# One more chunk by seven products, with operand sums made by transfers, and new due dates, in the last batch of an attention and feed-forward kernel

## The chip, the cores and the metric

The kernel runs on one core of a Trainium2 chip. Its matrix engine (TensorE, PE in the profile) multiplies a loaded 128 x 128 weight by a stream of columns and adds into banks of PSUM; each bank holds 128 rows of 512 numbers in 32 bits. VectorE (DVE) and ScalarE (ACT) read those banks; GpSimd (POOL) works within SBUF here and issues the loads from DRAM; SyncE (SP) issues the stores and the transposes. The metric is the device time of one execution in microseconds; the time before is the median of three executions.

## What the kernel computes

There are two stages. The first is cross-covariance attention over the channels, for B = 4 batches with N = 5824 tokens and C = 256 channels. The second is a feed-forward of d_ff = 1024 without any nonlinearity but a product of two linear maps.

```python
qn = q / (norm(q, axis=1) + 1e-06)          # along the 5824 tokens
kn = k / (norm(k, axis=1) + 1e-06)
s = kn.transpose(0, 2, 1) @ qn / tau        # 256 x 256 per batch
a = softmax(s, -1)
x = (v @ a).reshape(23296, 256)

h = (x @ w1) * (x @ w2)                     # 23296 x 1024
out = (h @ w3) @ w_out                      # w3: 1024 x 1024, w_out: 1024 x 256
```

The inputs and the output are float32; the kernel's matmuls take bf16 operands and add in 32 bits.

## The kernel before, in words

**The algebra.** Two products are folded ahead. w3 @ w_out becomes W_sb, 1024 x 256, once. For every batch a @ w1 and a @ w2 become Wf[b] (256 x 1024 each, index w = 0 and 1), once the batch's scores G = q^T k, the norms and the softmax are known. So what is left for a token is a = v Wf[b] w=0, b = v Wf[b] w=1, abh = a * b, and o = abh W_sb. While batch b is at this, the loads and scores of the next batch run between; the last batch, b = 3, has none beside it.

**Tiling.** A batch is cut into 12 chunks (c = 0 to 11) of 512 tokens, the last of 192 columns; d_ff is cut into 8 blocks (j = 0 to 7) of 128. v is turned by transposing transfers that SP issues, two chunks together (`turned_v`).

**The first product, block by block.** `normal` (L986 to L1022) takes one block of one chunk: 2 matmuls 128 x 512 for a and 2 for b (L993), a cast of a by ACT (`as`, L983) and a multiplication by DVE into the tile abh (L1015). In batch 3 the chunks go in pairs (0,1), (2,3), (4,5), (6,7), (8,9), and some blocks of a pair are made by `by_seven` (L1026 to L1075) instead: a product of 2 x 2 blocks with 7 multiplications in place of 8, so 7 matmuls 128 x 512 (L978; into banks named X, Y, T and Z) for two chunks' a and b. It takes sums of the weights (`wsum`, made once) and sums of tokens (`tsum`, four POOL operations per pair, `token_sum`, L680 to L686), and DVE does four operations for it, two of them additions out of the banks. `BY_SEVEN` (L552) says how many of the eight blocks of a pair go that way.

**The second product, chunk by chunk.** When all eight blocks of a chunk are done, `queue_out` queues its product with W_sb, in one of two forms. `plain_products` has 8 steps, each of 4 matmuls 128 x 256 (`emit_half`, L1087), copied out by two ACT operations in batch 3 and stored by one transfer on SP. `seven_products` (L756 to L884) uses the same trick of 7 for 8: 7 steps, each of 8 matmuls 128 x 128 (L828; banks prodA, prodB, prodC), sums of W_sb's quarters (`comb_T`), and four sums S of the chunk's own abh. POOL makes these four sums, 128 x 1024 each (L788 for the first, L790 for the others, in two tiles S0 and S1). ACT copies the products out (`keep`, L841; the copy that seeds prodB, L858), DVE adds to them (`join`, L848), and SP stores the chunk (L882). A list `PLAIN` (L554) says which chunks take the plain form; in batch 3 these are 0, 2, 6, 9 and 10. The last chunk, 11, is emitted block by block, and so is 10.

**A third form that is in the code but not in use.** For a chunk in `BY_DMA` (L555, empty) the four sums are made by transfers within SBUF: SP issues two plain copies (L806, L807) and POOL issues four transfers that add what they read to what they write (`by_transfer`, L798). The second and third wait for the first to land, the fourth waits for the third. Two of the additions write over parts of the chunk's own abh. Since a transfer can add but not subtract, this form works with other signs: three of the four sums of W_sb are taken negated (`comb_N`, three POOL operations of 128 x 512, `negate_weights`, L741), and for half of the chunk's rows ACT multiplies by -1 on the way out of the bank (L839) and DVE subtracts (L846).

**What sets the order.** The program of every engine is fixed when the kernel is built. `step` (L1406) plays the engines forward with estimated costs (`now`, `work_on`) and at each turn chooses among a `normal` block (its start plus `N_BIAS`), up to two `by_seven` blocks, and the next step of the second product (plus `O_BIAS`, when there is no hurry). POOL's work lies in a list; `pool_due` (L621) issues, of what may go, the item with the least due time. The due time of a chunk's sum is the number of steps of second products ahead of it times `STEP`; that of a token sum is `SLOT` times `TOKENS_AHEAD` blocks less `T_EARLY`. `plan` (L1376) lays out the blocks of a batch, and among them the places of the `by_seven` blocks and, `TOKENS_AHEAD` blocks before a pair, the place at which its token sums are queued. `LANDING` (2.8) is what the planner takes for a transfer within SBUF. POOL also issues the loads of v, each behind a small copy that waits for a block of the product (the gate).

Of the kernel before, what the change touches and what calls it, by code (L numbers as in the profile page):

```python
# [11 lines left out]
F32 = DT.float32  # L12
BF16 = DT.bfloat16

P = 128
# [2 lines left out]
BIG_BUFS = 31  # L18
HALF_BACK = 12
LANDING = 2.8  # L20
STEP = 1.55
SLOT = 1.45
T_EARLY = 1.0
N_BIAS = 0.04
O_BIAS = 0.15
MM_COL = 1.0 / 2400.0
MM_FIX = 0.0025

# [2 lines left out]
def kernel(  # L31
# [12 lines left out]
    nc = tc.nc  # L44
# [28 lines left out]
    work = ctx.enter_context(tc.tile_pool(name="work", bufs=2))  # L73
# [475 lines left out]
        )  # L549


    BY_SEVEN = {(3, 0): 3, (3, 2): 4, (3, 4): 4, (3, 6): 4, (3, 8): 4}  # L552
    PAIRED = {b: tuple(c for b2, c in sorted(BY_SEVEN) if b2 == b) for b in range(B)}
    PLAIN = {0: (0, 1, ), 1: (), 2: (), 3: (0, 2, 6, 9, 10, )}  # L554
    BY_DMA = {3: ()}  # L555
    TSUM, WSUM0, TSUM0 = 100, 12.0, 26.0
    wsums = {}
    tsums = {}
# [2 lines left out]
    now = {"PE": 0.0, "ACT": 0.0, "DVE": 0.0, "POOL": 0.0}  # L561
# [6 lines left out]
    def work_on(engine, cost, *after):  # L568

        now[engine] = max(now[engine], *after, 0.0) + cost  # L570
        return now[engine] + LATE[engine]
# [36 lines left out]
    def pool_add(due, item):  # L608

        pool_line.append((*item, due))  # L610

    def steps_until(key, step):

        n = step
        for line in outs:
            if line.key >= key:
                return n
            n += line.left
        return n
# [34 lines left out]
    def queue_token_sums(b, c):  # L654

        until = now["PE"] + TOKENS_AHEAD * SLOT

        def step(i):
            def fn(at_):
                token_sum(b, c, i)  # L660
                if i == 3:
                    tready[b, c] = at_
            return fn

        for i in range(4):
            pool_add(
                lambda i=i: until - now["PE"] + 1.1 * (i - 3) - T_EARLY,
                (0.0, lambda: turned_at.get((b, c // 2), FAR) <= now["PE"], 1.06, step(i)),
# [87 lines left out]
    def seven_products(b, c, k1, k2, whole):  # L756
# [8 lines left out]
        my_key = out_key(b, c)  # L765
        if c not in BY_DMA.get(b, ()):
            summed.append(line_key)
# [3 lines left out]
        def first_line():  # L771
            return min(summed) if (b, c ^ 1) in summed or c % 2 == 0 or (b, c - 1) in was or c - 1 in PLAIN.get(b, ()) else None

# [20 lines left out]
        def by_transfer(i):  # L794
            def fn(at_):
                s3, s2 = sums["t"][:, 0], sums["t"][:, 1]
                dst, src = {3: (s3, a21), 1: (a21, a22), 2: (s2, s3), 4: (a12, s2)}[i]
                nc.gpsimd.dma_start(out=dst, in_=src, accum_op=ALU.add)  # L798
                sums[i] = dst
                made[i] = at_ + LANDING  # L800
            return fn

        by_dma = c in BY_DMA.get(b, ())
        if by_dma:
# [5 lines left out]
            for i, allowed in (  # L810
# [5 lines left out]
                pool_add(  # L816
                    lambda i=i: steps_until(my_key, {3: 2, 1: 3, 2: 2, 4: 6}[i]) * STEP - {3: 7.5}.get(i, 4.0),
                    (whole, allowed, 0.55, by_transfer(i)),
                )
        for i in range(1, 1 if by_dma else 5):  # L820
            pool_add(lambda i=i: steps_until(my_key, {1: 2, 2: 2, 3: 4, 4: 6}[i]) * STEP - 2.1, (whole, (lambda i=i: (i == 1 and sums_live[0] < 2 and first_line() == line_key) or (i > 1 and i - 1 in made)), 2.1, sum_step(i)))

# [65 lines left out]
    def plain_products(b, c, ab2, whole):  # L888

        for i in range(FT):  # L890
            yield lambda i=i: max(out_bank(f"out{i // 4}", whole), w_made[0])
            emit_half(b, c, i, ab2)
# [22 lines left out]
    def out_key(b, c):  # L915
        return b, c + 1.5 * (c in BY_DMA.get(b, ()) and c in PAIRED[b])

    def put_out(b, c, gen, steps):
        line = Line(gen)
        line.key = out_key(b, c)  # L920
        line.left = steps
        k = len(outs)
        while k > 1 and outs[k - 1].key > line.key:
            k -= 1
        if k == 1 and outs[0].key > line.key and not outs[0].begun:
            k = 0
        outs.insert(k, line)
        steps_left[0] += steps

    def queue_out(b, c, whole):  # L930

        ab2 = tuple(halves[c])
        queued[b] = queued.get(b, 0) + 1
        if c in PLAIN.get(b, ()):
            put_out(b, c, plain_products(b, c, ab2, whole), FT)
# [90 lines left out]
    def by_seven(b, c, j):  # L1026

        W = Wf[b]
        js = slice(j * P, (j + 1) * P)
        yield lambda: max(  # L1030
            bank_at(4), wready.get(b, FAR), tready.get((b, c), FAR), whole_at(2)
        )
        T = tsums[b, c]
        S = [wsums[b][h][:, x, :] for h in range(2) for x in range(2)]
        xt, X = take(f"X_{b}_{c}_{j}", True)
        r = mm512(X, W[:, 0, 0, js], rhs_of(b, c, 0), True)
        yt, Y = take(f"Y_{b}_{c}_{j}", True, True)
        nc.scalar.copy(Y, X)
        copied = work_on("ACT", 0.475, r, free.get(yt, 0.0))
        yield lambda: bank_at()  # L1040
        tt, t = take(f"T_{b}_{c}_{j}")
        r = mm512(t, S[0][:, js], T[:, 0], True)
        t5 = work.tile([P, 512], F32, tag="t5", name=f"t5_{b}_{c}_{j}", bufs=2)
        nc.scalar.copy(t5, t)
        t5_at = free[tt] = work_on("ACT", 0.475, r)
        yield lambda: max(copied, whole_at(1))
        r = mm512(X, S[1][:, js], T[:, 1], False)
        zt, Z = take(f"Z_{b}_{c}_{j}", True, True)
        nc.vector.tensor_add(Z, X, t5)
        z_at = work_on("DVE", 0.607, r, t5_at, free.get(zt, 0.0))  # L1050
        yield lambda: copied
        r = mm512(Y, W[:, 1, 0, js], rhs_of(b, c, 1), False)
        a0 = cast(Y, f"as_{b}_{c}_{j}")
        a0_at = free[yt] = work_on("ACT", 0.475, r)
        held.discard(yt)
        yield lambda: z_at
        r = mm512(X, S[2][:, js], T[:, 2], False)
        b1 = work.tile([P, 512], BF16, tag="b_sb", name=f"bs_{b}_{c + 1}_{j}", bufs=2)
        nc.vector.tensor_add(b1, X, t5)
        b1_at = work_on("DVE", 0.61, r)  # L1060
        yield lambda: z_at
        r = mm512(Z, S[3][:, js], rhs_of(b, c + 1, 1), False)
        h1 = place(b, c + 1, j)
        nc.vector.tensor_mul(h1, two_halves(b1), two_halves(Z))
        free[zt] = work_on("DVE", 0.6, r, b1_at)
        held.discard(zt)
        finish(b, c + 1, j, free[zt])
        yield lambda: b1_at
        r = mm512(X, W[:, 1, 1, js], T[:, 3], False)
        h0 = place(b, c, j)  # L1070
        nc.vector.tensor_mul(h0, two_halves(a0), two_halves(X))
        free[xt] = work_on("DVE", 0.6, r, a0_at)
        held.discard(xt)
        last_ab[:] = [h0, free[xt]]
        finish(b, c, j, free[xt])  # L1075
# [95 lines left out]
    for nm in "kq":  # L1171
        new_piece(nm, 0, 0)
        raw[nm] = work.tile([P, half, C], F32, tag="o_sb", name=f"raw_{nm}", bufs=3)
        first = nc.sync if nm == "k" else nc.scalar
# [131 lines left out]
    def make_agenda(b):  # L1306
# [42 lines left out]
        if b == 0:  # L1349
            for i in range(4):  # L1350
                at(COMB + COMB_STEP * i, 0.0, lambda i=i: combine_weights(i))
        if b == min((m for m in BY_DMA if BY_DMA[m]), default=-1) - 1:
            at(90, 0.0, negate_weights)
# [22 lines left out]
    def plan(b):  # L1376

        todo, sevens = [], []
        c = 0
        if b == 0:  # L1380
            todo += [(c, h * 4 + j) for h in range(2) for c in range(2) for j in range(4)]
            c = 2
        while c < NCH:
            if c in PAIRED.get(b, ()):
                k = BY_SEVEN[b, c]
                mine = [(2 * i + 1) * FT // (2 * k) for i in range(k)]
                rest = [j for j in range(FT) if j not in mine]
                first = len(todo)
                todo += [(c + d, j) for j in rest for d in range(2)]
                n = len(todo) - first  # L1390
                sevens += [(first + max(0, i * n // k), c, j) for i, j in enumerate(mine)]
                if c > 0:
                    token_at[b, max(0, first - TOKENS_AHEAD)] = c
                c += 2
            else:
                todo += [(c, j) for j in range(FT)]
                c += 1
        return todo, sevens

    TOKENS_AHEAD = 5  # L1400
    token_at = {}
    stuck = [0]
    credit = [0.0]
# [2 lines left out]
    def step(b, todo, sevens, at_n):  # L1406
# [14 lines left out]
        if lines["N"] is not None:  # L1421
            choices.append((max(now["PE"], lines["N"].est()) + N_BIAS, 3, lines["N"]))
        if outs:
            hurry = credit[0] > 0.0 or steps_left[0] > 2 * HALF_BACK or not todo
            choices.append((max(now["PE"], outs[0].est()) + (-0.02 if hurry else O_BIAS), 4, outs[0]))
        if not choices:
# [25 lines left out]
    for b in range(B):  # L1452
# [3 lines left out]
        todo, sevens = plan(b)  # L1456
# [10 lines left out]
    n = len(ends)  # L1467
# [37 lines left out]
```

## Time and profile before

| | us |
|---|---|
| median of three executions (551.62 to 551.68) | 551.64 |
| the profiled execution | 551.72 |
| its span in the profile | 549.9 |
| PE busy | 539.4 |
| DVE busy | 421.4 |
| POOL busy | 405.0 |
| ACT busy | 396.5 |
| PE's weight loads busy | 351.2 |

The busy times are sums over the span; the weight loads run beside the matmuls. Matmuls of PE overlap in the profile, so that the mean time of one (379 ns for 128 x 512) is more than what one adds to the time; what one adds is read from the distance of two starts. The groups of rows by line tell which operation a time belongs to, since each operation of the second product has its own line: 2.13 us for one of POOL's sums (L788, L790), 0.37 us for a copy of a product by ACT (L841), 0.41 us for an addition by DVE (L848). No row of this profile shows a transfer that adds, or one from SBUF to SBUF that isn't a transpose.

### The profile page before, as it was taken

The numbers are of one execution on the slowest core, as the hardware profiler recorded it, in microseconds if no ns is written. First come the engines' busy times: TensorE is split into PE (matmuls) and PEld (weight loads), VectorE is DVE, ScalarE is ACT, GpSimd is POOL, SyncE is SP. The second block draws the span as 40 slices with busy tenths as digits, with TensorE's granted clock in tenths as the row PEclk, the third lists the DMA queues.
The fourth block names the chain that finished last, engine by engine and source line by source line (L and its number), as shares of the span: only waits on it lengthen the run. The fifth ranks groups of instructions, "written<-read, shape, count | busy, mean of one in ns | idle before, by whom it ended". The sixth has DMA issues, their size and how long they took to land.

```text
span 549.9 us, 12135 instructions
## 1 busy us (share of the span) xinstructions
PE 539.4 (98%) x4555; PEld 351.2 (64%) x4562; DVE 421.4 (77%) x741; ACT 396.5 (72%) x816; POOL 405.0 (74%) x332
## 2 busy tenths in 40 slices
PE   8799999999999999999999999999999999999996
PEld 4574566666677666666658666666667656666576
DVE  5577648999866888888766788888777787888861
ACT  5446648889777888888666888888777767677662
POOL 4270398479899399799987598969999746889460
PEclk9999999999999999999999999999999999999999
DMA  9999987985685748974673857766571334650113
GB/s 213 211 205 207 212 167 155 225 176 112 130 191 113 184 88 167 180 167 100 143 159 117 168 119 153 159 153 102 127 145 77 80 91 110 144 102 39 78 40 134
DMA packets 75018, 77.58 MB, mean 141 GB/s; under 512 B 54224, under 2 KB 58832, under 8 KB 74960
## 3 DMA queue, kind: packets, MB, share of 16 engines
q0 software_dynamic: 15664, 38.93, 40.6%
q1 hardware_dynamic: 58928, 37.17, 24.6%
q8 instruction: 35, 0.57, 0.4%
q10 hardware_dynamic: 368, 0.72, 0.4%
q14 instruction: 23, 0.19, 0.1%
HBM read 78.91 MB, written 23.86 MB: 187 GB/s over the span
## 4 chain that ended last, share of the span: by engine, by line
PE 93%; DMA 5%; ACT 1%; DVE 0%; issue 0%; POOL 0%; ACTq 0%; POOLq 0%
PE a L993 26%; PE b L993 26%; PE prodA L828 12%; PE prodC L828 6%; PE G L214 5%; PE o L1087 4%; PE X L978 3%; PE prodB L828 3%; DMA k<-in_k_dram 3%; PE fold L447 2%; DMA q<-in_q_dram 2%; PE o_out L1125 1%; PE w L1274 1%; PE T L978 1%; PE Y L978 1%; PE Z L978 1%
## 5 line engine op out<-in xcount | busy, mean ns | idle before, releaser
L1015 DVE TENSOR_TENSOR abh<-as,b 128x512 bf16<-128x512 bf16 x314 | 214.3, 685 | 75.5 <-ACT as L983 53.5
L983 ACT CAST as<-a 128x512 bf16<-128x512 f32 (+1 forms) x346 | 194.4, 563 | 67.3 <-PE a L993 53.7
L993 PE MATMUL a<-vT,Wf 128*128 128x512 bf16 x628 | 186.8, 379 | 0.1
L993 PE MATMUL b<-vT,Wf 128*128 128x512 bf16 x628 | 186.8, 379 | 0.0
L993 PEld LDWEIGHTS <-Wf 128*128 128x128 bf16 x1384 | 124.9, 98 | 80.5 <-issue 0.3
L788 POOL TENSOR_TENSOR S<-abh,abh 128x1024 bf16<-128x1024 bf16 x37 | 78.8, 2130 | 61.7 <-DVE abh L1015 51.6
L228 DVE TENSOR_TENSOR acc<-acc,sq 128x512 f32<-128x512 f32 x132 | 91.6, 694 | 2.3 <-ACT sq L211 1.0
L828 PEld LDWEIGHTS <-S 128*128 128x128 bf16 x1184 | 77.8, 98 | 22.2 <-POOL S L790 0.5
L790 POOL TENSOR_TENSOR S<-S,abh 128x1024 bf16<-128x1024 bf16 x37 | 79.2, 2141 | 2.6
L790 POOL TENSOR_TENSOR S<-abh,S 128x1024 bf16<-128x1024 bf16 x37 | 78.9, 2132 | 0.1
L790 POOL TENSOR_TENSOR S<-abh 128x1024 bf16<-128x1024 bf16 x37 | 78.8, 2130 | 0.1
L828 PEld LDWEIGHTS <-abh 128*128 128x128 bf16 x888 | 58.7, 98 | 19.2 <-issue 0.7
L841 ACT COPY osb<-prodA 128x256 f32<-128x256 f32 x111 | 41.3, 372 | 18.5 <-PE prodA L828 18.1
L214 PE MATMUL G<-k,q 128*128 128x256 bf16 x276 | 52.4, 273 | 0.0
L214 PEld LDWEIGHTS <-q 128*128 128x128 bf16 x276 | 27.0, 98 | 32.1
L828 PE MATMUL prodA<-comb_T,S 128*128 128x128 bf16 x592 | 45.1, 219 | 0.0
L211 ACT ACTIVATE sq<-q 128x512 f32<-128x512 bf16 x69 | 43.8, 635 | 0.1
L211 ACT ACTIVATE sq<-k 128x512 f32<-128x512 bf16 x69 | 43.5, 630 | 0.0
L848 DVE TENSOR_TENSOR osb<-osb,prodC 128x256 f32<-128x256 f32 x74 | 30.7, 414 | 4.3 <-ACT osb L841 3.3
L1087 PE MATMUL o<-W_sb,abh 128*128 128x256 bf16 x192 | 27.0, 273 | 0.0
L128 POOL DMA_DIRECT2D q<-in_q_dram x27 | 15.1, 561 | 12.0 <-DMA q<-in_q_dram 5.6
L1087 PEld LDWEIGHTS <-abh 128*128 128x128 bf16 x192 | 18.7, 98 | 7.9
(165 smaller groups left out, 622.2 us busy)
## 6 DMA issues: line engine op xcount, KB each, us to landing
out_dram<-osb SPq DMA_DIRECT2D x44, 512.0 KB, 3.5
k<-in_k_dram POOLq DMA_DIRECT2D x19, 512.0 KB, 8.7
v<-in_v_dram POOLq DMA_DIRECT2D x19, 512.0 KB, 7.6
q<-in_q_dram POOLq DMA_DIRECT2D x18, 512.0 KB, 5.4
w<-in_moe_w_dram POOLq DMA_DIRECT2D x4, 512.0 KB, 16.5
k<-in_k_dram POOLq DMA_DIRECT2D x4, 320.0 KB, 7.3
v<-in_v_dram POOLq DMA_DIRECT2D x4, 320.0 KB, 4.3
q<-in_q_dram POOLq DMA_DIRECT2D x3, 320.0 KB, 5.5
```

The lines of the kernel that those rows point to most:

```text
L211: nc.scalar.activation(out=sqs[0][:, :, part, :], in_=src[:, o : o + 2, :], func=AF.Square)
L214: nc.tensor.matmul(G[:, ct, :], lhsT=qt[:, i, ct * P : (ct + 1) * P], rhs=kt[:, i, :], start=(pr == 0 and part == 0 and ct == 0), stop=(pr ...
L228: nc.vector.tensor_add(accs[n], accs[n], sqs[0][:, part - 2])
L788: nc.gpsimd.tensor_add(x, a21, a22)
L790: nc.gpsimd.tensor_sub(x, *{2: (sums[1], a11), 3: (a11, a21)}.get(i) or (a12, sums[2]))
L828: nc.tensor.matmul(st[nm][:, i, :], lhsT=a[:, j, i * P : (i + 1) * P], rhs=w[j], start=(first and j == 0 and i == 0), stop=(j == 3), skip_ ...
L841: nc.scalar.copy(quarter(r, d), st[nm])
L978: nc.tensor.matmul(dst, lhsT=lhsT, rhs=rhs, start=start, stop=True, skip_group_check=True)
L983: nc.scalar.copy(a_sb[:, :n], t[:, :n])
L993: nc.tensor.matmul(t[:, :n], lhsT=Wf[b][:, ct, w, j * P : (j + 1) * P], rhs=rhs_of(b, c, ct), start=(ct == 0), stop=(ct == CT - 1),)
L1015: nc.vector.tensor_mul(ab, two_halves(a_sb), two_halves(t))
L1087: nc.tensor.matmul(t[:, k, :], lhsT=ab2[j // 4][:, h, j % 4, k * P : (k + 1) * P], rhs=W_sb[:, j, :], start=(j == 0 and k == 0), stop=(j = ...
```

## The change

In batch 3, chunk 6 goes from the plain form to that of seven products, with its sums by transfers (`PLAIN` without 6, `BY_DMA` with 6). In pair (4,5) three blocks instead of four go by `by_seven`, in pair (8,9) five instead of four. Six numbers of the planner change: `STEP`, `SLOT`, `T_EARLY`, `N_BIAS`, `O_BIAS` and `TOKENS_AHEAD`. `by_seven` gets a second way for one of its additions, b1, a copy by ACT and an addition by POOL, taken where the planner counts it as earlier by `B1_BIAS`, and the step behind it waits for X to be read instead of for b1 to be done. In `plan`, `max(0, ...)` goes, around a number that is never negative.

```diff
-STEP = 1.55
-SLOT = 1.45
-T_EARLY = 1.0
-N_BIAS = 0.04
-O_BIAS = 0.15
+STEP = 2.0
+SLOT = 1.2
+T_EARLY = -4
+N_BIAS = 0
+O_BIAS = 0.05
+B1_BIAS = -0.25
...
-    BY_SEVEN = {(3, 0): 3, (3, 2): 4, (3, 4): 4, (3, 6): 4, (3, 8): 4}
+    BY_SEVEN = {(3, 0): 3, (3, 2): 4, (3, 4): 3, (3, 6): 4, (3, 8): 5}
...
-    PLAIN = {0: (0, 1, ), 1: (), 2: (), 3: (0, 2, 6, 9, 10, )}
-    BY_DMA = {3: ()}
+    PLAIN = {0: (0, 1, ), 1: (), 2: (), 3: (0, 2, 9, 10, )}
+    BY_DMA = {3: (6, )}
...
         b1 = work.tile([P, 512], BF16, tag="b_sb", name=f"bs_{b}_{c + 1}_{j}", bufs=2)
-        nc.vector.tensor_add(b1, X, t5)
-        b1_at = work_on("DVE", 0.61, r)
+        by_vector = max(now["DVE"], r) + 0.61
+        through = max(max(now["ACT"], r) + 0.475, now["POOL"]) + 1.1
+        if through < by_vector + B1_BIAS:
+            u3 = work.tile([P, 512], F32, tag="u3", name=f"u3_{b}_{c}_{j}", bufs=2)
+            nc.scalar.copy(u3, X)
+            x_read = work_on("ACT", 0.475, r)
+            nc.gpsimd.tensor_add(b1, u3, t5)
+            b1_at = work_on("POOL", 1.1, x_read)
+        else:
+            nc.vector.tensor_add(b1, X, t5)
+            x_read = b1_at = work_on("DVE", 0.61, r)
...
-        yield lambda: b1_at
+        yield lambda: x_read
         r = mm512(X, W[:, 1, 1, js], T[:, 3], False)
...
-                sevens += [(first + max(0, i * n // k), c, j) for i, j in enumerate(mine)]
+                sevens += [(first + i * n // k, c, j) for i, j in enumerate(mine)]
...
-    TOKENS_AHEAD = 5
+    TOKENS_AHEAD = 2
```

The lines that make the sums by transfers are unchanged:

```python
        def by_transfer(i):
            def fn(at_):
                s3, s2 = sums["t"][:, 0], sums["t"][:, 1]
                dst, src = {3: (s3, a21), 1: (a21, a22), 2: (s2, s3), 4: (a12, s2)}[i]
                nc.gpsimd.dma_start(out=dst, in_=src, accum_op=ALU.add)
...
            nc.sync.dma_start(out=sums["t"][:, 0], in_=a11)
            nc.sync.dma_start(out=sums["t"][:, 1], in_=a22)
```

## The prediction, made before the change was run

> **What bounds the kernel now.** First the page: shares of the span by engine, and the chain that ended last.
>
> ```profile
> PE 539.4 (98%) x4555; PEld 351.2 (64%) x4562; DVE 421.4 (77%) x741; ACT 396.5 (72%) x816; POOL 405.0 (74%) x332
> PE 93%; DMA 5%; ACT 1%; DVE 0%; issue 0%; POOL 0%; ACTq 0%; POOLq 0%
> ```
>
> PE is busy for 98% and carries 93% of the chain; the DMA share lies in the start, before any work of this change. So a change pays if PE issues less, or waits less; the other engines count only where a sum, a cast or a bank comes late for PE.
>
> Then the sums by stretches, for the last batch, from the first step whose place changes to the last matmul:
>
> ```profile
> core 0: us, PE busy (x) PEld busy (x) DVE busy (x) ACT busy (x) POOL busy (x), PEclk, DMA share, GB/s
> 432.00:546.00 114.00, 113.67 (x911) 72.34 (x908) 87.23 (x148) 74.29 (x155) 72.39 (x52) 1.00 0.35 88
> ```
>
> The clock is full. Busy shares hide small waits, so I read PE's timeline by starts, not by durations:
>
> ```profile
> 515.45 0.60 PE L1087 MATMUL o<-W_sb,abh 128*128 128x256 bf16 x4
> 515.92 0.38 PE L978 MATMUL X<-tsum,wsum 128*128 128x512 bf16 x1
> 516.13 0.38 PE L978 MATMUL Z<-vT,wsum 128*128 128x512 bf16 x1
> 516.35 0.60 PE L1087 MATMUL o<-W_sb,abh 128*128 128x256 bf16 x4
> 516.78 0.38 PE L978 MATMUL X<-vT,Wf 128*128 128x512 bf16 x1
> ...
> 520.02 0.61 PE L828 MATMUL prodA<-W_sb,abh 128*128 128x128 bf16 x8
> 520.47 0.59 PE L993 MATMUL b<-vT,Wf 128*128 128x512 bf16 x2
> 521.13 0.38 PE L978 MATMUL X<-tsum,Wf 128*128 128x512 bf16 x1
> ```
>
> Start to start, eight matmuls of 128 columns take 0.45 us (56 ns each), four of 256 take 0.43 to 0.44 (109 ns), one of 512 takes 0.216, one of 192 takes 0.082 (medians over the execution). The pair of b at 520.47 should have ended at 520.90; X came at 521.13: a wait of 0.22. From 432.28 (the last matmul at the same place in both programs) on, PE issues 319 x 512, 184 x 256, 32 x 192 and 368 x 128 columns: 112.19 us at these medians. The last one ends its turn at 545.71, 113.43 later. So all waits of PE in this stretch come to 1.24 us: 0.08 at 432.5, 0.17 at 440.0, 0.18 at 458.0, 0.17 at 501.4, 0.22 at 520.7, 0.29 at 540.3, and crumbs. That is the ground to be won by reordering; there is no more.
>
> **The change, part by part.**
>
> *Chunk 6 by seven products.* It drops 8 steps of 4 matmuls with 256 columns (32 x 0.109 = 3.49 us) for 7 of 8 matmuls with 128 (56 x 0.056 = 3.13). Term: -0.36. The 24 extra weight loads are hidden: L828 has 56 ns per matmul with a new weight load each.
>
> At this place the Trainium skill speaks against the change: "TensorE: Matmul & The Clock Gate", section "Back-to-back issue gap", gives about 81 ns per matmul at 128 columns in a stream of weight loads and matmuls. By it the 56 products would take 4.54 us, and the term would be +1.05 against the plain step's measured 3.49. The trace shows 56 ns in every group of eight, so the sum takes 56.
>
> *One block by seven from pair 4 to pair 8.* 19 blocks stay 19; PE's count of 512-column matmuls is 319 in both. Term 0 on PE. DVE does four operations for such a block (685 ns each) instead of two, so 1.4 us of DVE work moves from 464-482 to 503-522. Chunk 6 adds 2 x 0.42 there, and on ACT five copies of 0.36 to 0.37 instead of two of 0.59 (+0.7). DVE was busy for 16.59 of 20 us between 500 and 520; with 2.2 more it is at some 94%. Cover: banks (four to six in a ring). Without cover PE waits as at 520.7; bounds below.
>
> *The new way for b1* (a copy by ACT, the addition by POOL) is taken by no block of the changed program: term 0. *Negated weights.* Three POOL operations of 128x512 stand before S0 of (2,7). No row has this form; bounds are 0.61 (L732, a cast) and 1.15 (L730), so 1.8 to 3.5 us. POOL sits idle 0.6 before its gate at 399.15 and 0.83 at 422.86; PE takes the sums of (2,7) to (2,10) 4.6 us or more after they end (S0 of (2,10) ends at 427.18, its product starts at 431.83). Term 0; without this cover, at most 3.5.
>
> *Due times.* They reorder POOL: both S1 sums of 3_1 and 3_3 now stand before the token sums, and those of pair 8 behind three sums of chunk 5.
>
> ```profile
> 484.33 2.12 POOL L788 TENSOR_TENSOR S<-abh,abh 128x1024 bf16<-128x1024 bf16 x1 [0.99 <-DVE abh L1071]
> ...
> 492.78 1.16 POOL L680 TENSOR_TENSOR tsum<-vT 128x512 bf16<-128x512 bf16 x1
> ...
> 497.36 2.13 POOL L788 TENSOR_TENSOR S<-abh,abh 128x1024 bf16<-128x1024 bf16 x1
> 499.56 2.13 POOL L790 TENSOR_TENSOR S<-S,abh 128x1024 bf16<-128x1024 bf16 x1
> ```
>
> Before, token sums at 492.78 push chunk 5's second sum to an end of 501.69, and PE waits for it (the 0.17). After, I put POOL's chain end to end, behind PE's matmuls laid end to end in the new order. The gate of the last v waits for a part whose matmul is at 480.29 and was at 480.14, so the two issues end at 483.3, as before; chunk 4 now closes with a b at 481.39, not with an X at 482.76, and no longer holds POOL until 484.33. Then four sums (492.78 - 484.33 = 8.45), three of chunk 5 (6.37), token sums (4.58), the last of chunk 5 (2.09), then S0 of chunk 7: second sum ends 483.3 + 21.49 + 2.20 + 2.13 = 509.1. PE wants it at 509.36. Slack 0.2, the tightest of POOL's; S1 of 3_5 ends 504.8 for 505.2. The v of pair 8 is issued behind both S0 of 3_3, 1.5 us later than 467.70; its token sums start at 498, so that costs nothing.
>
> *PE's waits.* Four go with the order: 0.08 and 0.18 (products now stand between two X that ran into each other), 0.17 (above), 0.22 (the last X of chunk 8 follows its third by 2.2 us instead of 1.5): -0.65. The 0.29 at the end stays, since both programs end with the same steps. New ones: none shown; bounds 0 and the 0.65 that vanish; I take 0.2, the size of the crumbs among the old waits (1.24 less the six named). Term: -0.45, from -0.95 (all but the end's) to 0.
>
> *Sums by transfer.* Two plain copies on SP (behind the store of chunk 4, before chunk 5's) and four adding transfers on POOL replace nothing on an engine. The first addition is issued behind S1 of 3_7, at 511.2. The second waits for its landing, and PE wants that second sum at 518.97, the third at 519.85, the fourth, which waits for the second and for prodB, at 524.0. With a time t from issue to landing: 511.3 + 2t = 518.97, so t may be 3.8. No adding transfer is in the trace. Nearest rows, quiet end of the run:
>
> ```profile
> out_dram<-osb SPq DMA_DIRECT2D x8, 512.0 KB, 2.6
> v<-in_v_dram POOLq DMA_DIRECT2D x1, 320.0 KB, 4.5
> v<-in_v_dram POOLq DMA_DIRECT2D x1, 32.0 KB, 2.0
> ```
>
> 256 KB lies between the store's rate (below 2.6) and POOL's own loads (2.0 + 224/288 x 2.5 = 3.9). Both ends are far from an addition, which reads twice; I take the middle, 3.1. Term 0; ends: 0, and +0.13 at 3.9 (each 0.1 beyond 3.8 costs 0.2). Loads of 512 KB take 6.1 here (v issued at 467.70, transposed at 473.76): 4.5 late for the second sum and 1.0 more for the fourth (511.4 + 3t against 524.0 and the first wait).
>
> The same skill, "DMA: Bandwidth & Descriptors", section "Anatomy of one DMA", would price 256 KB at 2.0 + 0.6 = 2.6 us, an estimate; no run here shows an addition.
>
> Behind each waiting transfer stands POOL's next work: S1 of 3_7 (between the first two, so it is issued in time, ends 513.9 for 514.39), and S0 of 3_8, needed at 527.9, held until chunk 8 closes near 523 anyway. On SP only stores wait.
>
> Sum: -0.36 - 0.45 = -0.81. The profiled execution takes 551.72 (span 549.9 and 1.8 around it), 0.08 over the median 551.64. Forecast 550.85 for the median.
>
> **Rivals.**
>
> *A, the transfers come late (slower).* PE stops at the first product with the negated weights. At t = 4.8 the wait is 1.9 and eats gain plus 0.2%; at 6.1 it is 5.5 and the time 556.3. For it: cast loads take 4.5 for 320 KB, and a store of chunk 7 falls into the same microseconds. Against it: DMA share there is 0.13.
>
> *B, the gain is eaten by POOL or DVE.* If chunk 4's sums start at 484.33 as before, S0 of 3_7 ends at 510.1, +0.8: 551.65. If all 2.2 us of DVE's added work between 503 and 522 lie on the path: 553.05. For: slack 0.2, and 94%. Against: chunk 4 closes 1.4 earlier, and DVE still idles over 1 us there.
>
> *C, all waits but the end's vanish*: -0.36 - 0.95, 550.3. For: the old order's waits were chance neighbours. Against: a greedy order makes new ones.
>
> *D, the reordering does nothing and only the products count*: 551.3. Against: 0.65 of waits have named causes.
>
> **How the numbers follow.** About 0.2% (1.1 us) is what a measurement can tell from no change: the lines are 550.54 and 552.74. Forecast, with 550.4 to 551.4 as its own range, 0.50 (0.18 of it below the lower line); A 0.26 (0.06 within); B 0.14 (0.10 slower, DVE's end); C 0.06; D 0.04. Faster 0.24, within 0.06 + 0.32 + 0.04 + 0.04 = 0.46, slower 0.20 + 0.10 = 0.30. The range runs from C to A at t = 4.9: 550.3 to 552.9; some 0.14 above and 0.04 below are left out.
>
> **What would show it.** Right: 319 matmuls of 512 in the stretch, 152 of 256 and 424 of 128; products at 56 ns; prodA_3_6 with S behind its neighbour without a gap; adding transfers landing within 3.8 us; no PE wait near 458, 501 and 521; POOL idle at 422 shortened, PE the same up to 432. Wrong: PE idle before the products of chunk 6 with a DMA as releaser, weight loads showing between 128-column matmuls, DVE as releaser of X between 503 and 522, or POOL's issues of the additions taking more than the 0.57 of a load.

## The result, and the profile after

The changed kernel takes 554.33 us (median of six executions, 553.85 to 555.68), the kernel before 551.66 beside it: a ratio of 1.005, with an interval of 1.0038 to 1.0061. It is slower by 2.7 us, where 550.85 was forecast, 0.8 below the kernel before. The profiled execution of after takes 554.06 us, its span is 552.1.

First the page of after, shares of the span by engine and the chain that ended last:

```profile
PE 539.1 (98%) x4586; PEld 350.6 (64%) x4586; DVE 424.1 (77%) x743; ACT 395.7 (72%) x819; POOL 412.6 (75%) x339
PE 90%; DMA 6%; DVE 1%; issue 1%; ACT 1%; POOL 0%; DVEq 0%; POOLq 0%
```

PE has 0.3 us less to do, its share of the chain is down from 93 to 90%, and a DMA share of 6% now holds a transfer within SBUF. The sums of the last batch (the stretch that answers to 432.00 to 546.00 of before, shifted by the 0.57 that this execution starts the last batch later, and 1.27 longer):

```profile
432.57:547.84 115.27, 113.27 (x935) 72.15 (x932) 88.37 (x150) 74.03 (x158) 77.71 (x57) 1.00 0.39 101
```

PE's idle time is 115.27 - 113.27 = 2.0 here against 0.33 before. PE's timeline shows nearly all of it in one place:

```profile
519.60 0.59 PE L994 MATMUL b<-vT,Wf 128*128 128x512 bf16 x2
521.69 0.62 PE L829 MATMUL prodA<-comb_N,S 128*128 128x128 bf16 x8 [1.49 <-DMA S<-S]
522.14 0.38 PE L979 MATMUL X<-tsum,wsum 128*128 128x512 bf16 x1
522.36 0.38 PE L979 MATMUL Z<-vT,wsum 128*128 128x512 bf16 x1
522.98 0.62 PE L829 MATMUL prodC<-comb_N,abh 128*128 128x128 bf16 x8 [0.24 <-DMA abh<-abh]
```

By starts, the pair of b at 519.60 should end its turn at 520.04; the product with the negated weights starts at 521.69, a wait of 1.65. The Z at 522.36 should end at 522.58, and prodC starts at 522.98: 0.40 more. Both end on adding transfers. How long these took, from the DMA issues between 480 and 550 (the last number is us from issue to landing):

```profile
out_dram<-osb SPq DMA_DIRECT2D x8, 512.0 KB, 2.7
S<-abh SPq DMA_DIRECT2D x2, 256.0 KB, 2.6
...
S<-abh POOLq DMA_DIRECT2D x1, 256.0 KB, 3.3
S<-S POOLq DMA_DIRECT2D x1, 256.0 KB, 5.7
abh<-abh POOLq DMA_DIRECT2D x1, 256.0 KB, 5.4
abh<-S POOLq DMA_DIRECT2D x1, 256.0 KB, 3.3
```

The first and the fourth addition took 3.3, close to the 3.1 that was forecast. The second and the third took 5.7 and 5.4. In time, the issues of POOL and SP and POOL's own work between them, from the timelines:

```profile
512.31 0.92 POOL L799 DMA_DIRECT2D S<-abh  x1
...
512.94 2.45 POOL L791 TENSOR_TENSOR S<-abh,S 128x1024 bf16<-128x1024 bf16 x1
...
515.92 0.90 POOL L799 DMA_DIRECT2D S<-S  x1 [0.53 <-DMA S<-abh]
...
516.85 0.34 SPq L883 DMA_DIRECT2D out_dram<-osb  x1
...
517.50 0.88 POOL L799 DMA_DIRECT2D abh<-abh  x1 [0.68 <-DVE Z L1050]
...
522.17 0.86 POOL L799 DMA_DIRECT2D abh<-S  x1 [3.79 <-DMA S<-S]
```

Chunk 7's store of 512 KB (L883) is issued 0.9 after the second addition and 0.7 ahead of the third. The two that took 3.3 had no store beside them.

The whole difference of the two profiled executions, in four parts. The stretch runs from the start of the last batch's first Z on wsum (431.62 before, 432.18 after) to the start of the last matmul.

| us | before | after | difference |
|---|---|---|---|
| start to that Z | 431.62 | 432.18 | +0.56 |
| stretch of the last batch | 113.98 | 115.26 | +1.28 |
| tail, from the last matmul to the end of the span | 4.31 | 4.71 | +0.40 |
| outside the span | 1.81 | 1.91 | +0.10 |

The stretch by starts: PE's issue -0.36 as forecast; the two waits on transfers +2.06; all other waits 0.80 instead of 1.24, so -0.44. The start, the tail and the time outside the span were in no term of the forecast.

### The profile page after: what moved, and what is told of

Read it like the earlier page. It is cut to its first block, busy times and chain, and to the rows that moved or that the text cites. A ratio compares the mean times of both kernels' runs of the same rounds, so it can differ in the third digit from the quotient of the medians.

```text
span 552.1 us, 12203 instructions
## 1 busy us (share of the span) xinstructions
PE 539.1 (98%) x4586; PEld 350.6 (64%) x4586; DVE 424.1 (77%) x743; ACT 395.7 (72%) x819; POOL 412.6 (75%) x339
## 4 chain that ended last, share of the span: by engine, by line
PE 90%; DMA 6%; DVE 1%; issue 1%; ACT 1%; POOL 0%; DVEq 0%; POOLq 0%
PE a L994 25%; PE b L994 25%; PE prodA L829 12%; PE prodC L829 6%; PE G L215 5%; PE o L1097 3%; PE prodB L829 3%; DMA k<-in_k_dram 3%; PE X L979 2%; PE fold L448 2%; DMA q<-in_q_dram 2%; PE o_out L1135 1%; PE w L1284 1%; DMA abh<-abh 1%; PE T L979 1%
## 5 line engine op out<-in xcount | busy, mean ns | idle before, releaser
L829 PEld LDWEIGHTS <-abh 128*128 128x128 bf16 x928 | 61.3, 98 | 20.9 <-DMA abh<-abh 0.7
L829 PE MATMUL prodB<-W_sb,abh 128*128 128x128 bf16 x304 | 23.2, 219 | 0.0
L829 PE MATMUL prodA<-W_sb,abh 128*128 128x128 bf16 x304 | 23.2, 219 | 0.0
```

The source lines that it names most:

```text
L829: nc.tensor.matmul(st[nm][:, i, :], lhsT=a[:, j, i * P : (i + 1) * P], rhs=w[j], start=(first and j == 0 and i == 0), stop=(j == 3), skip_ ...
```

## The experiments

Theory: the loss is the collision of the second and third addition with chunk 7's store; the products and the reordering bring what was forecast. Rivals: additions are slow in themselves when they read a sum just made, or run two at once; or the new due dates cost the time. For each run the stretch, the waits of PE in it (starts against the usual distance; where a matmul is missing from the records its 0.216 is taken off) and the tail are from its profile.

| run | median us | before beside it | ratio, interval | stretch | waits | tail |
|---|---|---|---|---|---|---|
| before | 551.66 | | | 113.98 | 1.24 | 4.31 |
| after | 554.33 | 551.66 | 1.005, 1.0038 to 1.0061 | 115.26 | 2.86 | 4.71 |
| 1 dates and block alone | 551.05 | 551.75 | 0.999, 0.9982 to 0.9999 | 113.28 | 0.53 | 4.29 |
| 2 chunk 6 alone | 552.16 | 551.75 | 1.0007, 0.9998 to 1.0016 | 114.01 | 1.61 | 4.72 |
| 3 late store | 551.91 | 551.75 | 1.0004, 0.9995 to 1.0013 | 113.58 | 1.18 | 4.70 |
| 4 sums by POOL | 552.37 | 551.75 | 1.0012, 1.0003 to 1.0021 | 114.64 | 2.24 | 4.29 |
| 5 late store, pieces, swap | 551.11 | 551.81 | 0.9986, 0.9978 to 0.9995 | 113.18 | 0.78 | 4.33 |
| 6 idle copies in before | 552.27 | 551.81 | 1.0003, 0.9994 to 1.0012 | 113.98 | 1.23 | 4.73 |
| 7 dates only | 551.22 | 551.81 | 0.9986, 0.9977 to 0.9994 | 113.51 | 0.76 | 4.32 |
| 8 block only | 552.31 | 551.81 | 1.0005, 0.9996 to 1.0014 | 114.46 | 1.72 | 4.33 |
| 9 after again | 553.56 | 551.67 | 1.0042, 1.0028 to 1.0056 | 115.86 | 3.46 | 4.72 |
| 10 after, third profile | 553.25 (one) | 551.67 | | 115.18 | 2.79 | 4.72 |

**1. Due dates and the moved block alone**, against the changed kernel:

```diff
-    PLAIN = {0: (0, 1, ), 1: (), 2: (), 3: (0, 2, 9, 10, )}
-    BY_DMA = {3: (6, )}
+    PLAIN = {0: (0, 1, ), 1: (), 2: (), 3: (0, 2, 6, 9, 10, )}
+    BY_DMA = {3: ()}
```

> This is the changed kernel with chunk 6 back in the plain form: due dates and blocks alone. Theory 1 (the transfers carry the whole loss, the reordering gives what was forecast): PE issues as much as before, its small waits in the last batch go from 1.24 to about 0.8 us as in the changed kernel, where those that end on no transfer come to 0.80, so 0.4 faster, near 551.2 against 551.65 before. Theory 2 (the new due dates themselves cost time, by POOL's sums coming late or by a later start of the last batch): the loss stays, 552.5 or more. Theory 3 (the reordering does nothing): 551.5 to 551.8.

551.05, 0.70 below the kernel before it, with the upper end of the interval just under 1. The waits fall from 1.24 to 0.53, further than to the 0.80 expected, since three waits of after on POOL (0.18, 0.12 and 0.08, see below) are one of 0.14 here. Theory 2 falls: the dates and the moved block cost nothing together, they are the gain.

**2. Chunk 6 by transfers alone**, with old dates, against the kernel before:

```diff
-    PLAIN = {0: (0, 1, ), 1: (), 2: (), 3: (0, 2, 6, 9, 10, )}
-    BY_DMA = {3: ()}
+    PLAIN = {0: (0, 1, ), 1: (), 2: (), 3: (0, 2, 9, 10, )}
+    BY_DMA = {3: (6, )}
```

> This is the kernel before with chunk 6 by seven products and transfers, and old dates and blocks. Theory 1 (transfers late): PE issues 0.36 us less, the old waits of 1.24 stay, and the product with the second sum waits for a transfer, 1 to 3 us, so 552.3 to 554.5. Theory 2 (the dates cost the time): no wait on a transfer worth naming, 551.2 to 551.5. Either way the additions are issued at other times than in the changed kernel; if the three of them that land before 522 take 3.3 us where no store runs beside them and 5 or more where one does, the collision with the store is the cause.

Theory 1's wait was a miss: PE waits for no transfer here, and the time is only 0.4 above before. One reason is PE's order: with the old dates the product that reads the second sum starts at 522.31, and the second addition is issued at 516.20, so even a landing after 5.7, at 521.9, would have been in time. The absence of the wait therefore says nothing on the collision. The landings do. The DMA issues between 495 and 545:

```profile
S<-abh POOLq DMA_DIRECT2D x1, 256.0 KB, 3.4
S<-S POOLq DMA_DIRECT2D x1, 256.0 KB, 3.4
abh<-abh POOLq DMA_DIRECT2D x1, 256.0 KB, 4.4
abh<-S POOLq DMA_DIRECT2D x1, 256.0 KB, 3.3
```

In this order the stores are issued at 514.24, 2.0 ahead of the second addition, and at 519.08, behind the third (517.78). The second addition, the same transfer as in after with the same tile just added to, lands in 3.4. So it isn't slow by itself. The third, with a store beside it, takes 4.4. What the products save (0.36) is lost to new waits in PE's order (1.61 in all instead of 1.24); the 0.4 is the tail.

**3. The store of chunk 7 behind that of chunk 6**, against the changed kernel:

```diff
-            nc.sync.dma_start(out=rows[:, 4 * c : 4 * c + 4, :], in_=st["o"])
+            store = lambda: nc.sync.dma_start(out=rows[:, 4 * c : 4 * c + 4, :], in_=st["o"])
+            if (b, c) == (3, 7):
+                late_stores.append(store)
+            else:
+                store()
+            if by_dma:
+                late_stores.pop()()
...
+    late_stores = []
```

> This is the changed kernel with one transfer moved: the store of chunk 7 (512 KB, issued at 516.85 between the second and the third addition) is issued behind that of chunk 6. Theory 1a (the second and third addition took 5.7 and 5.4 us because the store shared the DMA engines with them): they land in 3.3 to 4.0, the wait of 1.65 before prodA with the negated weights goes below 0.3, that of 0.41 goes too, and the time falls by 1.7 to 2.1 against the changed kernel, to 0.4 to 0.8 below before. Theory 1b (an addition that reads a tile just added to, or two additions at once, take over 5 us by themselves): the landings stay above 5, the wait stays above 1.2, and the time stays within 0.4 of the changed kernel, some 1.5 to 2.5 above before.

The DMA issues between 495 and 545, and PE at the place of the wait:

```profile
S<-abh POOLq DMA_DIRECT2D x1, 256.0 KB, 3.3
S<-S POOLq DMA_DIRECT2D x1, 256.0 KB, 3.8
abh<-abh POOLq DMA_DIRECT2D x1, 256.0 KB, 3.7
abh<-S POOLq DMA_DIRECT2D x1, 256.0 KB, 3.3
```

```profile
518.94 0.59 PE L1001 MATMUL b<-vT,Wf 128*128 128x512 bf16 x2
519.38 0.61 PE L829 MATMUL prodA<-comb_N,S 128*128 128x128 bf16 x8
519.82 0.38 PE L986 MATMUL X<-tsum,wsum 128*128 128x512 bf16 x1
520.04 0.38 PE L986 MATMUL Z<-vT,wsum 128*128 128x512 bf16 x1
520.64 0.62 PE L829 MATMUL prodC<-comb_N,abh 128*128 128x128 bf16 x8 [0.22 <-DMA abh<-abh]
```

One store moved, the order of all else on every engine stayed, and the second addition lands in 3.8 instead of 5.7; b and prodA stand 0.44 apart, no wait. Theory 1a holds for it, 1b falls, since the two additions still overlap. The third still comes 0.38 late (3.7, issued 1.6 behind the second). The stretch falls by 1.68, to 0.40 below before, and the median by 2.4, but the median stays 0.16 above before instead of 0.4 below it: the tail is 4.70, as in after, and the wait of 0.38 stayed.

**4. The same four sums by POOL**, against the changed kernel:

```diff
-    BY_DMA = {3: (6, )}
+    BY_DMA = {3: ()}
```

> This is the changed kernel with chunk 6 by seven products, its four sums made by POOL (2.13 us each, 8.5 more) instead of by transfers. Theory 1 (transfers late, everything else as forecast): no wait on a transfer; but POOL, end to end between 483 and 516 in the changed kernel, has 8.5 less 3.6 of issues more to do there, so that one or two products of chunk 6 or 7 wait for a sum for 0.5 to 2 us: 0.5 below to 1.5 above before. Theory 2 (the dates cost the time): 552.5 or more with waits that don't end on POOL's sums of chunks 6 and 7.

0.6 above before, as theory 1 said. PE's largest wait ends on POOL's fourth sum of chunk 7:

```profile
519.19 0.38 PE L979 MATMUL X<-tsum,wsum 128*128 128x512 bf16 x1
520.35 0.62 PE L829 MATMUL prodC<-W_sb,S 128*128 128x128 bf16 x8 [0.78 <-POOL S L791]
```

By starts that is 0.94. POOL works without a break from 482.8 to 522.4 here, and makes that sum behind three of chunk 6. So transfers are worth trying: in this order POOL has no room for four more sums. Another order was not tried.

**5. The late store, the copies in pieces, and two products swapped**, against run 3:

```diff
-            nc.sync.dma_start(out=sums["t"][:, 0], in_=a11)
-            nc.sync.dma_start(out=sums["t"][:, 1], in_=a22)
+            for x, src in ((0, a11), (1, a22)):
+                for j in range(4):
+                    nc.sync.dma_start(out=sums["t"][:, x, j], in_=src[:, j])
...
+        if by_dma:
+            yield lambda: out_bank("out0", made.get(3, FAR))
+            keep(1, 1, product("A", sums[3], t3))
+            yield lambda: out_bank("out1", made.get(1, FAR))
+            r2 = product("C", sums[1], t1, True)
+        else:
...
```

> This is the changed kernel with the late store of chunk 7, and two edits more: each of the two plain copies on SP is cut in four (eight transfers of 64 KB instead of two of 256, so that the last stores fall on the same semaphores of the eight in turn as in the kernel before), and of chunk 6's products the one with the third addition's sum (prodC) goes behind the next prodA. Theory (the tail of 0.4 comes from the turn of the semaphores that SP checks one by one at the end; the wait of 0.38 before prodC from the third landing): tail from the last matmul to the end of the span back from 4.70 to 4.3, no wait before prodC; 0.7 to 0.8 below the late store's 551.91, so 551.1 to 551.2. Rival (the tail belongs to the adding transfers, whose queue must be emptied): tail stays at 4.7, 551.5.

551.11, 0.70 below the kernel before beside it, interval 0.9978 to 0.9995, and 3.2 below the changed one. The tail is back to 4.33. The products run through:

```profile
518.79 0.59 PE L1008 MATMUL b<-vT,Wf 128*128 128x512 bf16 x2
519.22 0.61 PE L830 MATMUL prodA<-comb_N,S 128*128 128x128 bf16 x8
519.67 0.38 PE L993 MATMUL X<-tsum,wsum 128*128 128x512 bf16 x1
519.88 0.38 PE L993 MATMUL Z<-vT,wsum 128*128 128x512 bf16 x1
520.10 0.59 PE L1008 MATMUL a<-vT,Wf 128*128 128x512 bf16 x2
520.53 0.61 PE L830 MATMUL prodA<-comb_T,S 128*128 128x128 bf16 x8
```

The stretch is 113.18: 0.80 less than before. It is no better than run 1 by the medians, and only 0.10 by the stretch: 0.25 of the 0.36 that the products save goes back, since three waits on POOL's sums (0.19, 0.12 and 0.07) stand here for run 1's one of 0.14 and the waits come to 0.78 instead of 0.53.

**6. Two copies that nobody reads, in the kernel before:**

```diff
         queued[b] = queued.get(b, 0) + 1
+        if (b, c) == (3, 6):
+            idle = work.tile([P, 2, 2 * P], BF16, tag="idle", name="idle", bufs=1)
+            for x in range(2):
+                nc.sync.dma_start(out=idle[:, x], in_=ab2[x][:, 0, 0])
```

> This is the kernel before with two small copies within SBUF on SP (64 KB each), once chunk 6 is done; nobody reads what they write. Theory (turn of the semaphores): the tail from the last matmul to the end of the span goes from 4.31 to 4.7 and the time up by 0.4 to 0.5, without any adding transfer in the program. Rival (the tail and the 0.1 outside the span come from the adding transfers): no change, within 0.1 of before.

The stretch is the same to 0.01, the tail is 4.73 instead of 4.31, the median 0.46 higher (the interval of the ratio doesn't tell this from no change; the profile does). No adding transfer is in this program, so the tail isn't theirs. What SP does after its last issue is in the waits of SP (us in total, times, longest), first of before between 543 and 552, then of this run between 544 and 552:

```profile
SPq L1500 <- DMA out_dram<-osb: 1.8, 2, 1.2
```

```profile
SPq L1504 <- DMA out_dram<-oleft: 2.2, 2, 1.8
```

The records of SP's last instructions, times from the start of the last matmul; each asks one of the eight semaphores of the transfers that SP and ACT issue, in a fixed order, 108 to 118:

```
semaphore        108   109   112   113   114   115   116   118
before          1.15  1.21  1.27  1.33  1.95  3.23  3.29  3.41
idle copies     2.94  3.45  3.51  3.57  3.63  3.69  3.75  3.81
run 5           1.17  1.23  1.30  1.36  1.94  3.27  3.33  3.45
```

The transfers take these semaphores in turn. Before, the last three stores hold 116, 115 and 118, and the checks of the others are done while these fly. Two transfers more, and they hold 108, 109 and 118: SP comes to the last one that lands (3.45) with six checks left, 0.06 each. Run 5 has eight copies instead of two, a full turn, and the old tail. So the 0.4 goes with where the turn of eight stands at the end: two transfers more make it, eight more do not. Other numbers were not tried.

**7. Due dates only** (blocks by seven as before, chunk 6 plain), against run 1:

```diff
-    BY_SEVEN = {(3, 0): 3, (3, 2): 4, (3, 4): 3, (3, 6): 4, (3, 8): 5}
+    BY_SEVEN = {(3, 0): 3, (3, 2): 4, (3, 4): 4, (3, 6): 4, (3, 8): 4}
```

> This is the kernel before with the new due dates and biases only; chunk 6 plain, four blocks by seven in pairs (4,5) and (8,9) as before. If the dates make the gain of the first experiment (0.70 below before) and the moved block nothing, 550.9 to 551.2; if the moved block takes pressure off POOL ahead of chunk 5's second sum (closing chunk 4 earlier), half of the gain is lost, 551.3 to 551.5; if it makes it all, 551.7.

The stretch is 113.51: the dates give 0.47 of the 0.70, the block the rest; by the medians it is 0.59 and 0.70, which these runs don't tell apart.

**8. The moved block only**, in the kernel before:

```diff
-    BY_SEVEN = {(3, 0): 3, (3, 2): 4, (3, 4): 4, (3, 6): 4, (3, 8): 4}
+    BY_SEVEN = {(3, 0): 3, (3, 2): 4, (3, 4): 3, (3, 6): 4, (3, 8): 5}
```

> This is the kernel before with one block by seven moved from pair (4,5) to pair (8,9), old dates, chunk 6 plain. If DVE's 1.4 us more between 503 and 522 lie on the path, 552.2 to 553.2 and PE waits there that end on DVE; if banks cover them, 551.4 to 551.9.

552.31, at the lower end of the first case; the stretch is 0.48 longer. The largest new wait is 0.41 at 506.85, and it ends on a cast by ACT, not on DVE:

```profile
506.85 0.38 PE L978 MATMUL Y<-vT,Wf 128*128 128x512 bf16 x1
507.48 0.59 PE L993 MATMUL b<-vT,Wf 128*128 128x512 bf16 x2 [0.25 <-ACT as L983]
```

So the block costs with the old dates and gains with the new ones. The two edits aren't to be priced one by one.

**9 and 10. The changed kernel again**, without an edit, for two more profiles.

> This is the changed kernel once more, for the spread. Of the 2.67 us between the medians its profiled execution explains 1.27 in the last batch, 0.40 in the tail and 0.14 outside the span; 0.57 lay ahead of the last batch. Theory (that 0.57 is the chance of one execution's loads, as in other kernels that start the last batch 0.2 to 0.6 later and are as much above their own median, and the rest of the median's loss is the collision, which differs from run to run): the last batch's first Z starts anywhere between 431.3 and 432.3 and the second addition takes between 4.5 and 7 us to land. Rival (the change delays the start of the last batch): 432.1 or later again, with the same 5.7.

> As the run before it, a third profile of the changed kernel: the start of the last batch between 431.3 and 432.3 if it is chance, 432.1 or later if it is the change's; the second addition's landing 5 us or more behind its issue, and PE's wait before the first product with negated weights over 1 us, if the collision with the store is there in every run.

The last batch's Z starts at 432.12 and 431.44, so the late start does not come with the change (run 6, without any of it, has 432.25). The second addition takes 6.3 and 5.4, PE's wait for it 2.26 and 1.35. It is there in every profile, and its size differs from run to run. The issues of the last one between 495 and 545:

```profile
S<-S POOLq DMA_DIRECT2D x1, 256.0 KB, 5.4
abh<-abh POOLq DMA_DIRECT2D x1, 256.0 KB, 5.3
```

## Why the prediction was wrong

**The step that failed is "Sums by transfer: Term 0".** Its price for an addition was good: 3.3 where no store is beside it, against 3.1 taken. Its bound was right too: the second sum must be there 7.67 after the first issue, two times 3.8. The first took 3.3; the second took 5.7, since it flew beside a store of 512 KB. The forecast named this store in rival A and then put it aside with a DMA share of 0.13. That is a mean over 20 us, and of the kernel before, which has none of these additions (the DMA share is the last number but one):

```profile
505.00:525.00 20.00, 19.94 (x150) 12.19 (x149) 16.90 (x28) 12.90 (x26) 11.10 (x6) 1.00 0.13 54
```

By stretches of 2 us around the wait, the sums of after read otherwise:

```profile
515.00:517.00 2.00, 2.00 (x20) 1.13 (x19) 1.87 (x5) 1.61 (x4) 1.29 (x2) 1.00 0.13 23
517.00:519.00 2.00, 2.00 (x16) 1.06 (x14) 1.82 (x4) 1.71 (x5) 0.88 (x1) 1.00 0.88 175
519.00:521.00 2.00, 1.20 (x12) 0.59 (x10) 2.00 (x4) 1.16 (x3) 0.00 (x0) 1.00 1.00 291
521.00:523.00 2.00, 1.07 (x11) 0.58 (x12) 0.78 (x2) 0.37 (x1) 0.83 (x1) 1.00 0.37 62
```

Where the second and third addition and the store fly, the DMA engines are full, at 0.88 and 1.00. Run 3 moves the store alone and takes the wait away; that is shown. Rival A was the right mechanism with too little weight (0.26, where the forecast had 0.50), and its price was built on one time for all additions: 4.8 for each would make the wait 1.9. What came is 3.3 and 5.7, and 1.65. PE idle before the products of chunk 6, with a DMA as releaser, is among the signs of being wrong that the forecast listed.

Smaller errors lie on the same path. POOL's four sums of chunks 4 and 5 start at 484.46, 483.9 on the clock of before, and not at 483.3; the first addition goes out at 512.31, 511.7 on that clock, and not at 511.2. An addition holds POOL's queue for 0.6 to 0.9, not for the 0.57 of a load, another of the listed signs.

**A term was missing: the end of the program.** The forecast said that both programs end with the same steps. That holds for PE. But two transfers more on the queues turn the semaphores by two, which makes 0.40 (runs 5 and 6). Besides, the programs with additions take 1.90 to 1.93 outside the span in their profiled executions, all others 1.77 to 1.81; so 0.1 goes with them, and the cause stays open.

**Chunk 6 by seven products: -0.36.** Right. In the stretch the 128-column matmuls still stand 56 ns apart, so the rule in the Trainium skill's "TensorE: Matmul & The Clock Gate", section "Back-to-back issue gap" (about 81 ns) does not hold in this kernel's stream.

**PE's waits: -0.45.** Right in the sum, and in part by luck: 1.24 fell to 0.80, -0.44, the transfers' waits aside. Of the four that were to go, 0.08, 0.18 and 0.22 went; the one at 440, which was not among them, shrank from 0.17 to 0.07. The 0.17 on chunk 5's sums did not go: it is 0.18, on its last sum, and two new waits on POOL's sums of chunk 7 are 0.12 and 0.08. The 0.2 for new waits was said to be the size of the crumbs, but 1.24 less the six named waits is 0.13; the new ones came to 0.20 all the same. The slack of 0.2 that the forecast called POOL's tightest was not there. That is the small end of rival B; its other end, DVE, did not come, as none of the new waits ends on DVE.

**One block by seven, moved: 0.** Right with the new dates (run 7 against run 1), wrong with the old ones (run 8: 0.48 on the stretch).

**Negated weights: 0.** Right: PE starts the last batch no later than programs without them do (431.44 in run 10). The bounds were too low: the three operations take 1.51 each in after, 4.4 together (390.19 to 394.58), and not 1.8 to 3.5. The cover was enough for that.

**The sum.** -0.81 was forecast. Run 5, in which the transfers land in time and the semaphores keep their turn, has -0.80 on the stretch and -0.70 in the median. So the terms on PE were right in their sum. Between -0.81 and the +2.34 of the two profiled executions lie 3.15: 2.06 of waits on transfers, 0.40 of the tail, 0.10 outside the span, and 0.56 of a late start that is no part of the change. Run 10, whose last batch starts 0.18 earlier than before's, is 1.53 above before's profiled execution. What stays open is the spread of the changed kernel, 553.25 to 555.68 over its twelve executions: three profiles show the wait on the second sum as 1.35, 1.65 and 2.26, and no run shows the longest executions inside. The three longest (555.32, 555.38 and 555.68) are also the only ones with a mean granted clock under 0.998 (0.996 and 0.997) among all executions, of any of these kernels, whose clock is on record; whether the lower clock makes them longer, no run shows.

## What to carry to other kernels

Price a transfer that PE waits for by what else flies in those few microseconds, not by the DMA share of a long stretch: list every transfer issued within its flight, stores too, and move the ones that nobody waits for (here a single store, 1.7 us of the stretch). When an edit adds or removes transfers, read the end of the program: which semaphores the last stores hold, and how many checks follow the last landing. And an edit that adds work beside the bound (the block, chunk 6) pays only as far as the queues that feed it have room: runs 1 and 5 end at the same time, since waits on POOL's sums gave back most of what the products saved.

## What was not expected of the hardware

- Additions within SBUF of 256 KB land in 3.3 to 3.4 us with no store beside them. The two plain copies of the same size that SP issues in after take 2.9, issued 0.4 behind a store, and 2.3, with none near; the 2.6 in the rows is their median. The Trainium skill's "DMA: Bandwidth & Descriptors", section "Anatomy of one DMA", works out to an estimate of 2.6 for 256 KB issued by GpSimd; the additions, issued so, take 0.7 more.
- A few late packets can hold a whole transfer. In after, of the second addition's 128 packets of 2 KB 121 had started by 518.75, 2.8 behind its issue, and it landed at 521.64. Behind the 2 KB packets of an addition stand 16 packets of 4 bytes; of the second addition's, 15 start between 518.74 and 518.91 and the last one at 521.29. Just ahead, a packet of 16 KB of instructions took 1.08 us (from 516.54), and the store's first packet behind it 1.10 instead of 0.17; then packets of the addition started 0.33 apart (519.01, 519.34, 519.67, 519.99), with room for one of the store between two of them. In the three profiles of the changed kernel and in run 3:

```
                              after   run 9   run 10   run 3 (no store)
16 KB of instructions, us      1.08    1.29     0.99     0.97
longest packet of the store    1.10    1.59     0.77     none
second addition to landing     5.7     6.3      5.4      3.8
PE's wait for it               1.65    2.26     1.35     none
```

The trace does not name the DMA engine of a packet, and no run moves the fetch of the instructions. That one engine of the 16 carries the delay is what 120 + 1 of 128 packets and 15 of 16 suggest; that the fetch starts it is read from the order of the packets. Neither is shown. That the store makes most of it is shown by run 3, in which the same fetch takes 0.97 and the addition 3.8.
- Two copies of 64 KB whose result nobody reads lengthen the end of the program by 0.42 (run 6), through the turn of eight semaphores.
